# Four short loads of 1, 2, 4 and 8 rows on GpSimd's queue, between the loads of W1 and W2

## The chip, the cores and the metric

One core of a Trainium2 chip. The metric is device time in microseconds (us) of one execution; lower is better. The profile's span is about 1.8 us shorter than that time. Where two kernels are compared, their runs were made on one chip. A run's mean granted TensorE clock is given where it is not 1.00.

## The reference

Linear attention over 8 batches of 8 heads (576 tokens of width 64), then a two-layer feed-forward with ELU:

```python
q_s = softmax(q, axis=-1)            # per token
k_s = softmax(k, axis=2)             # over the sequence
kv  = einsum('bhsd,bhse->bhde', k_s, v)
x   = einsum('bhsd,bhde->bhse', q_s, kv)     # -> 4608 tokens x 512
h   = x @ w_in                               # 512 -> 2048
g   = where(h > 0, h, exp(min(h, 0)) - 1)
out = g @ w_out                              # 2048 -> 512
```

## The kernel before

Tokens go through the feed-forward in nine blocks of 512. W1 and W2 are `w_in` and `w_out`; a unit of q, k or v is four of the eight heads of a batch. In each block, eight "hidden groups" of 256 hidden units are computed on TensorE into four pairs of PSUM banks; ScalarE takes the exp, an engine takes min(exp, 1), VectorE combines both into G and so frees the PSUM pair; then come the output matmuls. A small list scheduler in the program orders each engine's queue by estimated times.

```python
def hg(self, j, g, ps, key, how, kcs=(0, 1, 2, 3)):      # hidden group g of block j
    self.hg_mm(j, g, ps, kcs, key)                       # TensorE into PSUM pair ps
    # ... ScalarE: esb = exp(P) ...
    elif how == "gp":
        S.add("gp", 1120, lambda e: e.tensor_scalar(     # GpSimd: the minimum
            esb[:, :], esb[:, :], 1.0, 0.0, ALU.min, ALU.max), ...)
        S.add("dve", t_dve(1024), lambda e: e.scalar_tensor_tensor(   # VectorE: G, frees P
            gt, esb[:, :], -1.0, P[:, :], ALU.add, ALU.max), ...)
    else:                                                # VectorE: minimum, then G
        S.add("dve", t_dve(1024, 2), lambda e: e.tensor_scalar(...), ...)
        S.add("dve", t_dve(1024), lambda e: e.tensor_tensor(...), ...)

# in program(): GpSimd issues q, k, v of the first units, then W1 (16 pieces), then
for what in (0, "2q", "3q", 1, 2, "2k", "2v", "3k", 3, "3v", 4, 5):
    if isinstance(what, int):
        gp = self.load_w2(what, -50, follow=gp)          # W2 in 6 pieces
    # ... else q, k, v of units 2 and 3 ...

order = [A, Bs, C, Dd]                                   # the four PSUM pairs
for g in range(8):
    self.hg(j, g, order[g % 4], key, "gp" if j or g > 2 else "act" if g == 1 else "dve", ...)
# then the output matmuls; in block 0, W2 piece by piece; the key-value product of
# units 2 and 3 stands in the TensorE queue after the fourth W2 piece
```

In block 0 the minimum of group 3 is the first computing instruction on GpSimd after its loads, and group 7 reuses group 3's PSUM pair. (The four letters A to Dd are PSUM pairs; TensorE's queue is in program order.)

The softmax here doesn't subtract the row's maximum and nothing guards it: scores larger than these inputs give would overflow.

Of the kernel before, what the change touches and what calls it, by code (L numbers as in the profile page):

```python
# [6 lines left out]
F32 = mybir.dt.float32  # L7
# [4 lines left out]
B, H, S, D = 8, 8, 576, 64  # L12
# [245 lines left out]
class Gen:  # L258
# [13 lines left out]
    def alloc(self):  # L272
        nc = self.nc
        a = nc.alloc_sbuf_tensor
        self.ID = a("ID", [128, 128], F16)
        self.IDLE = a("IDLE", [128, 512], F32)
        self.W1 = a("W1", [128, 4, DFF], F32R)
        self.W2 = a("W2", [128, 16, 512], F32R)
        self.GT = a("GT", [128, 16, BLK], F32R)
        self.XT = a("XT", [128, 4, RING], F32R)  # L280
        self.ESB = [a(f"ESB{i}", [128, 1024], F32) for i in range(4)]
        self.OSB = [a(f"OSB{i}", [128, 512], F32) for i in range(4)]
        self.RAW = [{t: a(f"{t.upper()}R{i}", [128, 2, CH, D], F32) for t in "kv"}
                    for i in range(2)]
        self.RQ = [a(f"QR{i}", [128, 2, CH, D], F32) for i in range(4)]
        self.VB = [a(f"VB{i}", [128, 2, CH, D + 1], BF16) for i in range(2)]
        self.QS = [a(f"QS{i}", [128, CH, 128], F16) for i in range(2)]
        self.qsT = [a(f"qsT{i}", [128, CH, 128], F32R) for i in range(2)]
        self.MB = a("MBLK", [128, 2, 2, 128], F32R)
        self.MBLK = [self.MB[:, i, :, :] for i in range(2)]  # L290
        self.ZQ = [a(f"ZQ{i}", [128, 2, CH], F32) for i in range(2)]
        self.RZQ = [a(f"RZQ{i}", [128, 2, CH], F32) for i in range(2)]
        self.RZ = a("RZK", [128, 2, 2], F32)
        self.RZK = [self.RZ[:, i, :] for i in range(2)]
        self.SEEN = a("SEEN", [16, 4, 16], F32)
        self.PS = [nc.alloc_psum_tensor(f"PS{i}", [128, 1024], F32) for i in range(4)]

    def bank(self, i):
# [442 lines left out]
    def program(self):  # L741
        S = self.S
# [5 lines left out]
        for n, h in ((0, 0), (0, 1), (1, 0), (1, 1)):  # L748
# [6 lines left out]
                       follow=gp if eng == "gp" else sp, tag=f"ld q{n}")  # L755
            op.late = 1300 if n == 0 else 2000
            if eng == "gp":
                gp = op
# [4 lines left out]
        for n, t in ((0, "k"), (0, "v"), (1, "k"), (1, "v")):  # L763
            gp = self.load(n, t, "gp", -80, follow=gp)
            gp.late = 2350 if n == 0 else 2200 if t == "k" else 1850
        for s in range(4):
            gp = self.load_w1(s, -60, follow=gp)
# [24 lines left out]
        self.hg_mm(0, 1, 2, (1,))  # L792
        self.ao_rest(0, 1, -60)
        for what in (0, "2q", "3q", 1, 2, "2k", "2v", "3k", 3, "3v", 4, 5):
            if isinstance(what, int):
                gp = self.load_w2(what, -50, follow=gp)
            elif what == "3v":
                for h in range(2):
                    gp = self.load_half(3, "v", h, -50, gp)
            else:  # L800
                gp = self.load(int(what[0]), what[1], "gp", -50, follow=gp)
# [135 lines left out]
```

## Time and profile before

| | before |
|---|---|
| time, median of 2 runs | 298.34 us (298.19 to 298.48) |
| TensorE busy, of a span of 296.5 us | 98% |
| GpSimd: handling of the last load done / first minimum done | 24.84 / 25.93 us |
| TensorE: group 7 / outputs of block 0 / key-value product begin | 27.61 (the prediction worked out 27.53) / 29.43 / 43.07 us |

TensorE sets the end, so only what delays TensorE counts. For a load, the trace of GpSimd gives a start (the issue) and a duration up to the end of its handling on GpSimd. Those ends follow each other one at a time; their distances (0.53 to 0.99 us per load in the kernel before) are the queue's real pace. The prediction shows the lines.

One more line of the waits of the kernel before (who waited for whom: total us, times, longest us) is needed later. The prediction had not used it:

```profile
PEld PS L700 <- DMA W<-in_moe_w_out_dram: 0.4, 1, 0.4
```

It is a weight load of the output matmuls that waited 0.4 us for a piece of W2.

### The profile page before, as it was taken

What the parts mean: (1) busy time and instruction counts of PE and PEld (TensorE: products, weight loads), DVE (VectorE), ACT (ScalarE), POOL (GpSimd) and SP (SyncE); (2) the same over time, 40 slices, a digit from 0 to 9 for tenths busy, and PEclk for the clock granted to TensorE, in tenths of its full rate; (3) what the DMA queues carried; (4) which work ended last, traced back from release to release, by engine and by line L of the source; (5) the groups of instructions that cost most, each with busy time, mean ns of one, the idle gap of its engine ahead of it and who ended that gap; (6) DMA issues with size and microseconds to landing.
All of it is one profiled execution on the core that took longest, in us unless ns stands there. A gap on an engine that the chain in (4) does not pass through costs nothing.

```text
span 296.5 us, 4336 instructions
## 1 busy us (share of the span) xinstructions
PE 290.1 (98%) x1824; PEld 234.9 (79%) x1824; DVE 149.9 (51%) x167; ACT 151.9 (51%) x176; POOL 122.9 (41%) x133
## 2 busy tenths in 40 slices
PE   7999999999999999999999999999999999999995
PEld 2578778887888788878888888888888888888883
DVE  6757942988347903792268416760661056106600
ACT  5666367953676275536554555536531454135411
POOL 8998101662187035713472337314740055005500
PEclk9999999999999999999999999999999999999999
DMA  7999988928991597039902990099003110230022
GB/s 243 320 393 390 389 281 308 389 83 133 337 248 66 200 354 147 0 96 362 238 7 56 359 270 17 4 346 194 0 0 71 45 30 0 56 76 13 0 71 71
DMA packets 36515, 49.37 MB, mean 167 GB/s; under 512 B 16656, under 2 KB 17168, under 8 KB 36496
## 3 DMA queue, kind: packets, MB, share of 16 engines
q1 hardware_dynamic: 29792, 34.29, 40.7%
q0 software_dynamic: 6320, 14.29, 15.8%
q10 hardware_dynamic: 384, 0.53, 0.5%
q8 instruction: 14, 0.23, 0.3%
q14 instruction: 5, 0.04, 0.0%
HBM read 36.70 MB, written 9.44 MB: 156 GB/s over the span
## 4 chain that ended last, share of the span: by engine, by line
PE 84%; DMA 7%; POOL 7%; issue 0%; ACT 0%; DVE 0%; POOLq 0%
PE PS L700 41%; PE PS L654 39%; DMA VR<-in_v_dram 7%; POOL W L347 3%; PE PS L491 2%; PE PS L584 2%; PE PS L618 1%; POOL W L358 1%; POOL KR L315 1%; POOL VR L315 1%; POOL QR L315 0%; POOL QR L753 0%; ACT OSB L714 0%; DVE VB L442 0%; POOL ID L729 0%
## 5 line engine op out<-in xcount | busy, mean ns | idle before, releaser
L683 DVE SCALAR_TENSOR_TENSOR GT<-ESB,PS 128x1024 fp32r<-128x1024 f32 x69 | 84.1, 1221 | 115.7 <-POOL ESB L680 115.5
L700 PE MATMUL PS<-W,GT 128*128 128x512 f32 x576 | 136.5, 392 | 0.0
L654 PE MATMUL PS<-XT,W 128*128 128x512 f32 x576 | 132.9, 390 | 0.0
L654 PEld LDWEIGHTS PS<-XT,W 128*128 128x128 f32 x576 | 107.9, 188 | 22.7 <-DVE GT L676 0.4
L700 PEld LDWEIGHTS PS<-W,GT 128*128 128x128 f32 x576 | 107.0, 188 | 22.4 <-DMA W<-in_moe_w_out_dram 0.4
L680 POOL TENSOR_SCALAR ESB<-ESB 128x1024 f32<-128x1024 f32 x69 | 73.6, 1076 | 101.0 <-ACT ESB L668 101.0
L668 ACT ACTIVATE ESB<-PS 128x1024 f32<-128x1024 f32 x72 | 73.8, 1028 | 51.3 <-PE PS L654 51.3
L714 ACT ACTIVATE OSB<-PS 128x512 f32<-128x512 f32 x36 | 21.4, 600 | 61.3 <-PE PS L700 60.9
L438 POOL CAST VB<-VR 128x1152 bf16<-128x1152 f32 x12 | 14.5, 1210 | 45.4 <-DMA VR<-in_v_dram 45.4
L398 DVE TENSOR_REDUCE ZQ<-QR 128x18 f32<-128x1152 f32 (+1 forms) x18 | 21.8, 1214 | 2.5 <-ACT QR L392 2.5
L412 DVE TENSOR_TENSOR QS<-QR,RZQ 128x1152 f16<-128x1152 f32 x16 | 21.6, 1362 | 0.4
L392 ACT ACTIVATE QR<-QR 128x1152 f32<-128x1152 f32 (+1 forms) x18 | 18.5, 1053 | 2.1 <-DMA QR<-in_q_dram 2.0
L432 ACT ACTIVATE KR<-KR 128x1152 bf16<-128x1152 f32 x14 | 15.9, 1169 | 6.0 <-DMA KR<-in_k_dram 6.0
L425 POOL CAST qsT<-QR 128x1152 fp32r<-128x1152 f16 x12 | 13.8, 1147 | 10.1 <-DMA QR<-QS 10.1
L604 ACT ACTIVATE XT<-PS 128x640 fp32r<-128x640 f32 (+1 forms) x12 | 8.2, 738 | 15.4 <-PE PS L584 15.4
L358 POOL DMA_DIRECT2D W<-in_moe_w_out_dram x6 | 10.2, 2389 | 0.0
L347 POOL DMA_DIRECT2D W<-in_moe_w_in_dram x16 | 10.0, 1361 | 0.0
L640 PE MATMUL PS<-IDLE 128*128 128x512 f32 (+1 forms) x14 | 8.1, 702 | 1.5 <-DVE IDLE L732 1.5
L628 ACT ACTIVATE XT<-PS 128x1024 fp32r<-128x1024 f32 (+3 forms) x8 | 6.8, 846 | 1.1 <-PE PS L618 1.1
L584 PE MATMUL PS<-qsT,MBLK 128*128 128x320 f32 (+3 forms) x32 | 7.1, 338 | 0.0
L640 PEld LDWEIGHTS PS<-IDLE 128*128 128x128 f32 (+1 forms) x14 | 2.6, 211 | 5.5 <-issue 2.3
L491 PEld LDWEIGHTS PS<-VB,KR 64*64 64x64 bf16 x504 | 4.7, 107 | 2.8 <-DVE GT L683 1.8
(45 smaller groups left out, 82.2 us busy)
## 6 DMA issues: line engine op xcount, KB each, us to landing
out_dram<-OSB SPq DMA_DIRECT2D x68, 128.0 KB, 3.6
QR<-in_q_dram SPq DMA_DIRECT2D x12, 576.0 KB, 7.9
KR<-in_k_dram SPq DMA_DIRECT2D x12, 576.0 KB, 5.6
VR<-in_v_dram SPq DMA_DIRECT2D x12, 576.0 KB, 6.6
W<-in_moe_w_in_dram POOLq DMA_DIRECT2D x16, 256.0 KB, 9.5
W<-in_moe_w_out_dram POOLq DMA_DIRECT2D x3, 1024.0 KB, 16.9
KR<-in_k_dram POOLq DMA_DIRECT2D x4, 576.0 KB, 13.6
VR<-in_v_dram POOLq DMA_DIRECT2D x4, 288.0 KB, 14.6
```

Source lines behind the costliest of these rows:

```text
L347: "gp", 530, lambda e, kc=kc: e.dma_start(self.W1[:, kc, sl], w[kc, :, :, sl]), key,
L392: lambda e, part=part: e.activation(part, part, AF.Exp), key,
L398: S.add("dve", 1350 if n > 1 else 750, lambda e, z=z, src=src: e.tensor_reduce(z, src, AX.X, ALU.add), key, R=self.q_res(n) if n > 1 else ...
L412: S.add("dve", 1400, lambda e: e.tensor_tensor(qso, raw[:, :, :, :], rz, ALU.mult), key, R=qR + [f"RZQ{i}"], W=[f"QS{al}"], low=True, tag= ...
L432: S.add("act", t_act(1152, False), lambda e: e.activation(ek[:, :, :, :], flat.rearrange("p (h c d) -> p h c d", h=2, c=CH), AF.Exp), key, ...
L438: self.cv[n] = S.add("gp", 1250, lambda e: e.tensor_copy(VB[:, :, :, 0:D], raw[:, :, :, :]), key, R=rv, W=[f"VB{i}0", f"VB{i}1"], low=True ...
L654: last = e.matmul(P[:, t * 512:(t + 1) * 512], self.W1[:, kc, tt * 128:(tt + 1) * 128], self.XT[:, kc, rc:rc + BLK], start=(kc == 0), stop ...
L668: S.add("act", t_act(1024, True), lambda e: e.activation(esb[:, :], P[:, :], AF.Exp), key, W=[f"E{i}"], X=self.banks(ps), tag=f"exp{j}.{g}")
L680: S.add("gp", 1120, lambda e: e.tensor_scalar(esb[:, :], esb[:, :], 1.0, 0.0, ALU.min, ALU.max), key, X=[f"E{i}"], tag=f"min{j}.{g}", port ...
L683: S.add("dve", t_dve(1024), lambda e: e.scalar_tensor_tensor(gt, esb[:, :], -1.0, P[:, :], ALU.add, ALU.max), key, R=[f"E{i}"], W=gw, X=se ...
L700: last = e.matmul(dst, GT[:, jj, ts * 128:(ts + 1) * 128], self.W2[:, jj, :], start=(jj == 0), stop=(jj == 15))
L714: S.add("act", t_act(512, True), lambda e: e.activation(osb[:, :], src, AF.Copy), key, W=[f"O{i}0", f"O{i}1"], X=[f"b{bk}"], tag=f"evo{jb} ...
```

## The change

The edit adds four small transfers of different shapes on GpSimd's queue, before the first piece of W2. Nobody reads what they bring. It is a probe: what do four loads of next to no bytes do to a kernel whose first 45 us are full of loads?

```diff
@@ alloc
         self.SEEN = a("SEEN", [16, 4, 16], F32)
+        self.ROW = a("ROW", [8, 1152], F32)
@@ program
         for what in (0, "2q", "3q", 1, 2, "2k", "2v", "3k", 3, "3v", 4, 5):
+            if what == 0:
+                for i, (rows, n, at) in enumerate(((1, 384, 0), (2, 320, 384), (4, 256, 704), (8, 192, 960))):
+                    gp = S.add("gp", 600, lambda e, at=at, rows=rows, n=n: e.dma_start(
+                        self.ROW[0:rows, at:at + n], self.w_out[0:rows, 0:n]), -50, W=[f"ROW{i}"],
+                        dma=f"row{i}", nbytes=rows * n * 4, follow=gp, tag=f"row{i}")
             if isinstance(what, int):
                 gp = self.load_w2(what, -50, follow=gp)
```

## The prediction

> **What bounds the kernel now.** I read the page first: engine shares, then the slices, then the chain of work that ended last.
>
> ```profile
> PE 290.1 (98%) x1824; PEld 234.9 (79%) x1824; DVE 149.9 (51%) x167; ACT 151.9 (51%) x176; POOL 122.9 (41%) x133
> GB/s 243 320 393 390 389 281 308 389 83 133 337 248 66 200 354 147 0 96 362 238 7 56 359 270 17 4 346 194 0 0 71 45 30 0 56 76 13 0 71 71
> PE 84%; DMA 7%; POOL 7%; issue 0%; ACT 0%; DVE 0%; POOLq 0%
> ```
>
> TensorE carries the span, with the granted clock full in every slice. After some 45 us nothing holds it: the waits of the window from 45 us to the end give TensorE no wait of its own, and its weight loads sum to 2.2 us over six waits. So time lost before 45 us is not won back, and time lost elsewhere costs nothing. The change sits in the first 45 us, where the loads run at 389 to 393 GB/s in slices 3 to 5 (7.4 us each) and GpSimd issues all of them but two. The timeline of GpSimd, in small windows, shows the issuing. Columns: start, duration, engine, line, what.
>
> ```profile
> 5.69 0.65 POOL L347 DMA_DIRECT2D W<-in_moe_w_in_dram  x1
> ...
> 13.54 2.11 POOL L347 DMA_DIRECT2D W<-in_moe_w_in_dram  x1
> 14.06 2.35 POOL L358 DMA_DIRECT2D W<-in_moe_w_out_dram  x1
> 14.80 2.32 POOL L315 DMA_DIRECT2D QR<-in_q_dram  x1
> ...
> 22.35 2.49 POOL L358 DMA_DIRECT2D W<-in_moe_w_out_dram  x1
> 23.26 2.67 POOL L680 TENSOR_SCALAR ESB<-ESB 128x1024 f32<-128x1024 f32 x1
> ```
>
> Starts and ends differ: the sixteen W1 loads start 0.52 us apart but end 0.62 us apart ((13.54 + 2.11) - (5.69 + 0.65) = 9.31 us over 15). By the last, issue runs 2.11 us ahead of completion. The completions are thus the queue that limits GpSimd, and it never empties until W2's last piece at 22.35 + 2.49 = 24.84 us. The first minimum (of hidden group 3) starts at 23.26 us but takes 2.67 us where its sisters take 1.04: 24.84 + 1.04 = 25.88, near its end at 25.93. It waited for the load queue. This is the place that the change pushes.
>
> Who waits for that minimum? The timelines of VectorE and TensorE, and two of the waits:
>
> ```profile
> 25.97 3.48 DVE L683 SCALAR_TENSOR_TENSOR GT<-ESB,PS 128x1024 fp32r<-128x1024 f32 x3 [1.74 <-POOL ESB L680]
> ```
> ```profile
> 22.06 7.10 PEld L654 LDWEIGHTS PS<-XT,W 128*128 128x128 f32 x32 [0.40 <-DVE GT L676]
> ```
> ```profile
> 29.43 6.78 PE L700 MATMUL PS<-W,GT 128*128 128x512 f32 x28
> 36.04 0.68 PE L464 MATMUL PS<-ID,QS 128*128 128x128 f16 x9
> 36.53 2.98 PE L700 MATMUL PS<-W,GT 128*128 128x512 f32 x12
> 39.35 0.68 PE L464 MATMUL PS<-ID,QS 128*128 128x128 f16 x9
> 39.83 2.98 PE L700 MATMUL PS<-W,GT 128*128 128x512 f32 x12
> 43.07 0.78 PE L491 MATMUL PS<-VB,KR 64*64 64x65 bf16 x72 [0.26 <-DVE VB L442]
> ```
>
> VectorE had idled 1.74 us for GpSimd, then finished group 3 at 25.97 + 1.22 = 27.19 us. By the code, group 7's matmuls take the PSUM pair that this frees. The 32 matmuls of groups 4 to 7 begin at about 22.09 us at 0.227 us each, so group 7 begins at 22.09 + 24 x 0.227 = 27.53 us. The pair was free only 0.34 us earlier; a handover takes 0.05 us (a cast ended at 43.02, its reader began at 43.07), leaving **0.3 us of slack**. TensorE then runs without gaps until 43.07, where it waits 0.26 us for the last half of V of unit 3.
>
> [...] Differences between successive ends give 0.53 to 0.62 us for most loads of 128 pieces (W1, quarter-MB W2, half of V), 0.71 to 0.73 for 256 pieces (q, k, v), 0.76 to 0.99 for 512 (1 MB of W2). It is flat, but half a microsecond per load is not small here.
>
> [...]
>
> **The change part by part.** Nothing is removed. Added are four issues between the last W1 load and the first W2 load, a destination tile of 1152 floats that no one reads, and four semaphores that no one waits for.
>
> 1. Bytes: (384 + 640 + 1024 + 1536) x 4 = 14.3 KB, or 0.04 us at 390 GB/s. [...]
>
> 2. Generation time: from 128 to 256 pieces costs 0.15 us, so about 0.42 us remain for a load of almost no pieces; if the cost is flat below 128 it is 0.55. Four: 1.7 to 2.2 us. I take **1.9 us**. The issue starts shift by about the same.
>
> 3. Transfers: W2's first piece is issued 1.9 us later. It needed 13.4 us from issue to landing at 14.06 us, waiting behind W1:
>
> ```profile
> W<-in_moe_w_out_dram POOLq DMA_DIRECT2D x1, 1024.0 KB, 13.4
> W<-in_moe_w_in_dram POOLq DMA_DIRECT2D x3, 256.0 KB, 11.0
> ```
>
> A 1 MB load is 2.7 us of transfer at 390 GB/s, so most of those 13.4 us are backlog. The queue does not run dry when issue slips 1.9 us. The landings of W2, q, k, v of units 2 and 3 stay put to 0.1 us, including V at 42.5 us.
>
> 4. GpSimd's first minimum ends 1.9 us later, at 27.8. VectorE's group 3 ends at 29.1. Group 7 begins at 29.15 instead of 27.53: TensorE loses 1.9 - 0.3 = 1.6 us. It ends at about 31.0. Group 4's evacuation is done at about 30.3 and group 5's near 31.5, ahead of the output tiles that need those banks (31.0 and 32.8), so no second loss follows.
>
> 5. TensorE reaches the key-value product 1.6 us late, where it waited 0.26 us for V, which lands when it did: about 0.3 us come back. Net **1.3 us**, kept to the end: 298.34 + 1.3 = 299.64, rounded to 299.7 for small matters of item 1.
>
> 6. VectorE from 30.0 to 38.1 us is nearly full, with groups 6 and 7 and the softmax of q for units 2 and 3. It starts 1.9 us late and regains some of it in its former waits; the transposes at 36.04 and 39.35 us also move 1.6 us later, with 0.8 and 1.2 us spare before (the products end at 35.2 and 38.1). I expect no new wait.
>
> **The rivals.**
>
> A. Hidden. The shift is absorbed, as GpSimd is busy only 41% overall and no one reads the new tile: 298.3. For it: deep backlog of transfers. Against: the 1.74 us wait of VectorE for GpSimd right behind the loads, and only 0.3 us of slack.
>
> B. Small loads are dear to generate[...]. For: nothing measured; against: the flatness of the other loads.
>
> C. [...] If the 17 us from 27.5 to 44.5 grew by 5%, V and W2's tail would land 0.85 us later; with TensorE already 1.3 us late this is still hidden. Only over 8% would add to the sum, and 15% would make 301.0.
>
> D. Another order. The program sorts each engine's queue by estimated times, and the four loads enter it at 0.6 us each. A low-priority exp or reduction on ScalarE or VectorE may go ahead of an urgent one; one displaced softmax step is 1.2 to 1.4 us on those engines. It might cost up to that on TensorE, or save a part of the loss: 299 to 301.
>
> **Range and chances.** Generation between 0.3 and 0.55 us gives a loss of 0.6 to 1.6 us; rivals B and D stretch it upward. So 298.6 to 301.5 holds it 8 times in 10, around 299.7. Two per cent is 6 us: slower by that needs 1.7 us per small load or a lost overlap, 3%. Faster by 2% would need TensorE work to vanish, 1%. Within 2%: 96%.
>
> **What would show it.** Between the last W1 and the first W2 completion on GpSimd stand four issues of 0.4 to 0.55 us each; the first minimum ends near 27.8 us; VectorE's wait before its group 3 grows from 1.74 to about 3.6 us; the weight loads or matmuls before group 7 show a wait of about 1.6 us for VectorE; the output matmuls begin near 31.0 us; the 0.26 us wait at the key-value product is gone; V still lands near 42.5 us; the rest is the same, later. It is wrong if the first minimum moves by under 1 or over 3 us, if the loads land later by over 1 us, or if TensorE shows new waits after 45 us.

1.9 us on GpSimd, less 0.3 of slack, less 0.3 given back at V, is 1.3 us, so 298.34 + 1.3 = 299.64, put at 299.7. Gone are an allowance in item 1 that only the rounding up could draw on, the size of rival B (an assumption, measured nowhere, from which the range took a part of its upper end) and the cause that rival C gave for slower transfers; the shares by which C lets them slow are assumed. "Generation", here and in the expectations, is the time between the ends of two loads that follow each other on GpSimd; what GpSimd does in that time was not shown.

## The result and the profile after

299.24 us (299.19 to 299.28, 2 runs) against 298.34: a ratio of 1.0033, 95% interval 1.0009 to 1.0057, about +1.0 us. Ratios here are the mean time of one kernel's fast runs over that of the other's of the same rounds, so they differ a little from the ratio of the medians. By the 2% rule this is "the same"; the interval says that it is a small loss. It lies within the predicted range of 298.6 to 301.5, 0.5 us under the predicted 299.7.

GpSimd's timeline after (lines moved down by one in the file, from the new tile on):

```profile
13.57 2.13 POOL L348 DMA_DIRECT2D W<-in_moe_w_in_dram  x1
14.09 2.12 POOL L798 DMA_DIRECT2D ROW<-in_moe_w_out_dram  x1
...
15.61 2.10 POOL L798 DMA_DIRECT2D ROW<-in_moe_w_out_dram  x1
16.10 2.40 POOL L359 DMA_DIRECT2D W<-in_moe_w_out_dram  x1
...
24.52 2.07 POOL L359 DMA_DIRECT2D W<-in_moe_w_out_dram  x1
25.26 2.42 POOL L681 TENSOR_SCALAR ESB<-ESB 128x1024 f32<-128x1024 f32 x1
```

The last W1 load ends at 15.70, the last short load at 17.71: 2.01 us for four, **0.50 us each**. The queue ends at 26.59 (24.84 before), the first minimum at 27.68 (25.93). VectorE and TensorE, after:

```profile
27.71 4.61 DVE L684 SCALAR_TENSOR_TENSOR GT<-ESB,PS 128x1024 fp32r<-128x1024 f32 x4 [3.66 <-POOL ESB L681]
```
```profile
28.99 2.11 PE L655 MATMUL PS<-XT,W 128*128 128x512 f32 x8 [1.44 <-DVE GT L684]
30.94 6.51 PE L701 MATMUL PS<-W,GT 128*128 128x512 f32 x28
37.29 0.68 PE L465 MATMUL PS<-ID,QS 128*128 128x128 f16 x9
...
43.99 0.78 PE L492 MATMUL PS<-VB,KR 64*64 64x65 bf16 x72
```

The bracket on TensorE is new: group 7 waits 1.44 us for VectorE, which waited 3.66 us (1.74 before) for GpSimd. Now take the lag of each row against the kernel before: group 7 +1.38 us (28.99 against 27.61), outputs +1.51 (after the pause the eight matmuls took 1.95 us to the first output, before 1.82), first transpose +1.25 (37.29 against 36.04), key-value product +0.92 (43.99 against 43.07). The loss shrinks in two places. The first 28 output matmuls took 6.51 us instead of 6.78: that is the wait for W2 shown above, gone. And the wait of 0.26 us before the key-value product is gone. From there on the lag stays (the spans differ by 297.4 - 296.5 = 0.9 us). The chain that ended last names the same links (start, us, what):

```profile
15.69 2.01 POOL ROW L798 x4
...
25.33 1.26 POOL W L359 x2
26.59 1.10 POOL ESB L681
...
27.71 1.23 DVE GT L684
...
28.99 2.11 PE PS L655 x8
```

### The profile page after: what moved, and what is told of

It reads as the page before. It is cut to its first block, busy times and chain, and to the rows that moved or that the text cites. A ratio compares the mean times of both kernels' runs of the same rounds, so it can differ in the third digit from the quotient of the medians.

```text
span 297.4 us, 4340 instructions
## 1 busy us (share of the span) xinstructions
PE 289.4 (97%) x1824; PEld 234.7 (79%) x1824; DVE 149.6 (50%) x167; ACT 152.1 (51%) x176; POOL 124.7 (42%) x137
## 4 chain that ended last, share of the span: by engine, by line
PE 89%; POOL 9%; DVE 0%; issue 0%; ACT 0%; POOLq 0%
PE PS L701 45%; PE PS L655 40%; POOL W L348 3%; PE PS L492 2%; PE PS L585 2%; POOL W L359 1%; PE PS L619 1%; POOL KR L316 1%; POOL ROW L798 1%; POOL VR L316 1%; POOL QR L316 1%; POOL QR L754 0%; DVE GT L684 0%; POOL ESB L681 0%; POOL VR L337 0%
## 5 line engine op out<-in xcount | busy, mean ns | idle before, releaser
L641 PE MATMUL PS<-IDLE 128*128 128x512 f32 (+1 forms) x14 | 7.4, 632 | 1.9 <-DVE IDLE L733 1.5
```

## The experiments

Theory: each short load costs GpSimd half a microsecond of handling whatever its rows; this delays the first minimum, the freeing of a PSUM pair and group 7; waits for transfers later give about 0.6 us back. Rivals: the bytes or the odd row counts cost; a later arrival of W2 and V costs; the program's own scheduler reordered something. All twelve runs gave correct results; "GpSimd" below is the end of the first minimum, "group 7" the start of its matmuls, both from the profiled run.

| kernel | median, us | before, us | ratio (95%) | GpSimd | group 7 |
|---|---|---|---|---|---|
| the change (first result) | 299.24 | 298.34 | 1.0033 (1.0009-1.0057) | 27.68 | 28.99 |
| two loads | 298.35 | 298.04 | 1.0006 (0.9994-1.0017) | 26.86 | 28.17 |
| eight loads | 303.05 | 298.04 | 1.0160 (1.0144-1.0176) | 29.50 | 30.82 |
| rows on SyncE | 298.00 | 298.04 | 0.9998 (0.9985-1.0012) | 25.71 | no wait |
| rows behind W2 | 299.43 | 298.04 | 1.0045 (1.0031-1.0060) | 27.91 | 29.22 |
| order of before | 298.88 | 297.86 | 1.0034 (1.0021-1.0046) | 27.57 | 28.88 |
| 16 rows each | 298.86 | 297.86 | 1.0031 (1.0017-1.0045) | 27.51 | 28.82 |
| group 3 on VectorE, change | 298.01 | 297.86 | 1.0001 (0.9989-1.0014) | | no wait |
| group 3 on VectorE, before | 297.73 | 297.86 | 0.9993 (0.9981-1.0006) | | no wait |

### How many loads: two and eight

```diff
-  enumerate(((1, 384, 0), (2, 320, 384), (4, 256, 704), (8, 192, 960)))
+  enumerate(((4, 256, 704), (8, 192, 960)))                  # two
+  enumerate(((1, 384, 0), ..., (8, 192, 960)) * 2)           # eight; the second four into rows 8 to 15 of a taller tile
```

> Only the loads of 4 and 8 rows, on GpSimd's queue. Theory (generation time of about 0.5 us per load on GpSimd, TensorE held at group 7): the first minimum ends near 26.7 us, about 1 us earlier than with four; TensorE loses about 0.4 us before group 7, and the two waits for transfers that the kernel before had (0.6 us) swallow it: 298.3 to 298.5, no change from before. Rival (cost in proportion to the number of loads): half of +0.9, so 298.8. Rival (the load of one row alone is what costs): 298.3 too, but with the first minimum where it was before.

> The four loads twice over, eight in all. Theory: the queue of GpSimd ends 4 us later than before, the first minimum near 29.7 us, group 7 at about 31.0 us where it began at 27.5; 3.5 us lost, 0.6 given back: +2.9 us, about 301.2. Rival (in proportion): +1.8, about 300.1. Rival (a one-off[...]): +0.9, 299.2.

Two loads cost 0.0006 x 298 = 0.2 us, an interval that includes none. The minimum moved by 0.93 us and group 7 waited:

```profile
28.17 2.11 PE L655 MATMUL PS<-XT,W 128*128 128x512 f32 x8 [0.84 <-DVE GT L684]
...
43.17 0.78 PE L492 MATMUL PS<-VB,KR 64*64 64x65 bf16 x72
```

Yet the key-value product begins at 43.17 (43.07 before). Half the loads don't cost half the loss: the waits for transfers swallow the first 0.6 us.

Eight loads were my clearest miss: +4.8 us, not +2.9. GpSimd did as expected (29.50 for "near 29.7"; eight loads in 3.94 us, 0.49 each), and group 7 too (30.82 for "about 31.0"). But then:

```profile
30.82 3.58 PE L655 MATMUL PS<-XT,W 128*128 128x512 f32 x8 [2.50 <-DVE GT L684]
34.24 6.55 PE L701 MATMUL PS<-W,GT 128*128 128x512 f32 x28
```

Eight matmuls took 3.58 us instead of 2.11. Stretches of the same profile (busy times of the engines, then the granted TensorE clock, the third number from the end):

```profile
29.00:30.00 1.00, 0.00 (x0) 0.00 (x0) 0.46 (x1) 0.97 (x2) 1.00 (x4) 1.00 1.33 389
...
31.00:32.00 1.00, 1.00 (x3) 0.81 (x4) 1.00 (x2) 1.00 (x1) 1.00 (x2) 0.50 1.38 387
...
33.00:34.00 1.00, 1.00 (x4) 0.71 (x4) 1.00 (x2) 0.00 (x0) 0.00 (x0) 0.50 1.46 398
34.00:35.00 1.00, 1.00 (x6) 0.82 (x5) 1.00 (x2) 0.56 (x1) 0.00 (x0) 0.98 1.18 392
```

After a pause of 2.5 us TensorE was granted half its clock until 34.03 us. That is 1.5 us more. For the profiled run the sum then closes: 3.2 at group 7, plus 1.5, less 0.6, is 4.1 us, and it took 302.29 - 298.04 = 4.25 us more. The other three runs took 0.7 to 1.1 us longer still; no profile shows where. The section "More pauses" below looks at when the clock changes. All four runs of this kernel have a mean clock of 0.994. The changed kernel's pause of 1.44 us left the clock full.

### The bytes or the engine that issues them: rows on SyncE

```diff
-  gp = S.add("gp", 600, lambda e, ...: e.dma_start(...), ..., dma=f"row{i}", follow=gp, ...)
+  sp = S.add("sp", 600, lambda e, ...: e.dma_start(...), ..., dma=f"orow{i}", follow=sp, ...)
```

(The name with an o makes the program wait for them at its end.)

> The same four loads issued by SyncE, GpSimd's queue as before. Theory: the cost is GpSimd's time, not the bytes or the reads: 298.3, GpSimd's first minimum at 25.9 us. Rival (the transfers themselves disturb the DMA engines): +0.5 or more. The rows travel early here, before the W2 loads, so this does not exclude a disturbance that only loads from GpSimd make.

298.00 against 298.04: no cost; the first minimum ends at 25.71 and V is waited for again (0.22 us). The bytes are not it.

### Where the queue is delayed: rows behind W2

```diff
         for what in (0, "2q", ...):
-            if what == 0: ... the four loads ...
         self.ldq, self.w2 = None, [gp]
+        ... the four loads, after the last piece of W2 ...
```

> The four loads behind the last W2 load instead of ahead of the first. Theory: the first minimum waits for the same number of generations: the same as the changed kernel, +0.9, 299.2, and W2 lands as before or earlier. Rival (the delay of W2's and V's loads is what costs): 298.3.

+1.3 us, as high as the change or higher (the intervals overlap). W2's issues are not delayed at all here, so a late arrival of W2 or V can't be the cause. Here the minimum moved by the full 1.98 us, against 1.75 with the loads in front. The 0.23 us between is taken up below.

### The order of the queues, and the shape of the loads

Set beside the kernel before, the change also moved one reduction on VectorE and one cast on GpSimd by two places near 55 us. To take that away, the loads are counted at 1 ns in the scheduler's estimate; the queues then have the order of before:

```diff
-                    gp = S.add("gp", 600, lambda ...
+                    gp = S.add("gp", 1, lambda ...
```

> The four loads as in the change, but counted at 1 ns each in the program's own ordering of its queues, so that every engine's queue is in the order of the kernel before, save for the four loads. Theory: +0.9, 299.2. Rival (the displaced reduction on VectorE and cast on GpSimd near 55 us matter): nearer to 298.3.

The ratio is 1.0034, that of the change. The order is not it. And with 16 rows per load and the same bytes:

```diff
-  ((1, 384, 0), (2, 320, 384), (4, 256, 704), (8, 192, 960))
+  ((16, 24, 0), (16, 40, 24), (16, 64, 64), (16, 96, 128))
```

> Four loads of 16 rows each with the same bytes as the short ones[...]. Theory (fixed generation time, whatever the rows): +0.9, 299.2, 0.5 us per load in GpSimd's queue. [...]

(A rival: if the odd row counts cost, the time would be near 298.3.)

The ratio is 1.0031, 1.96 us for the four (0.49 each). The odd row counts are not it: one row or sixteen, a load takes GpSimd half a microsecond.

### Taking the link out: group 3's minimum on VectorE

```diff
-  self.hg(j, g, ..., "gp" if j or g > 2 else "act" if g == 1 else "dve", ...
+  self.hg(j, g, ..., "gp" if j or g > 3 else "act" if g == 1 else "dve", ...
```

> The changed kernel with the minimum of hidden group 3 moved from GpSimd to VectorE, which had been idle there for 3.7 us. Theory: group 7 no longer waits; the whole 0.9 us goes: 298.3, with the waits for W2 and V back. Rival (something else in the load queue costs): stays near 299.2.

> The kernel before with the same move. Theory: nothing to gain, as TensorE had 0.3 us of slack there and then waits for W2 and V anyway: 298.3, within 0.2 us. If the group 3 hand-over had a hidden cost before, this is faster by up to 0.5 us.

With the four loads and this edit, 298.01 against 297.86, ratio 1.0001: the whole loss is gone, though the loads are still issued. TensorE has no pause before group 7, and the two waits are back:

```profile
29.20 6.70 PE L701 MATMUL PS<-W,GT 128*128 128x512 f32 x28
...
42.74 0.78 PE L492 MATMUL PS<-VB,KR 64*64 64x65 bf16 x72 [0.22 <-DVE VB L443]
```

The same edit on the kernel before gives 0.9993, with 1 inside the interval: no gain shown, so no version that beats both. In the kernel before, the transfers hold TensorE next: 0.27 us for W2 in the first outputs and 0.26 us for V.

### More pauses: six loads, and eight with group 3 on VectorE

```diff
+  enumerate((..., (8, 192, 960), (1, 384, 0), (2, 320, 384)))   # six
   # and: the eight loads with the edit of the last section
```

> Six short loads (the four, then those of one and two rows again). With eight, TensorE's clock fell to half after a pause of 2.5 us, which no theory had counted. Theory with the clock holding: GpSimd's first minimum ends near 28.8 us, group 7 begins near 30.2 instead of 27.5, 2.6 us lost, 0.6 given back, +2.0 us (300.1), pause of about 2 us. If a pause of 2 us is enough to halve the clock: 1.5 us more, +3.5 (301.6).

> The kernel of six short loads once more, for a profile: of its six runs, five took 301.7 to 302.3 us, while the profiled one took 300.5 and had its slow clock at the start instead. Theory: in a profile of the usual kind TensorE pauses about 2 us before group 7 and then runs group 7 and the first outputs at half clock for some 3 us, and the time is about 301.8. Rival: the usual runs lose those 1.5 us elsewhere, and the clock after the pause is full.

> Eight short loads with the minimum of group 3 on VectorE. Theory: GpSimd's first minimum is now that of group 4, ends near 29.5 us as with eight loads, and its evacuation at about 30.8 releases the first output bank; group 7 is not held, the outputs begin near 30.9 instead of 29.4: 1.5 us lost, 0.6 given back, +0.9 (298.9), the pause 1.4 us and the clock full. If the halved clock came from the loads and not from the pause, the clock falls here too and the time is above 300.

Six loads, eight runs. One run with a full clock took 299.98, against 297.94 for the kernel before: +2.0, the theory's sum. Five took 301.7 to 302.3 at a mean clock of 0.994. Two took 300.5 (clock 0.992 and 0.994), and as luck had it, both of them were the profiled ones. These show neither reading of mine. In both, as the stretch of the second one's profile below has it with a clock of 0.66, TensorE had its slow clock between 10 and 15 us, long before group 7, and began the main part of block 0 at 19.3 us instead of 16.4, so that group 7 did not wait at all.

```profile
10.00:15.00 5.00, 5.00 (x35) 2.43 (x35) 3.25 (x7) 2.83 (x4) 5.00 (x12) 0.66 1.20 342
```

The two traces show how that came about. SyncE's second load of q, issued at 1.21 us as in every kernel, landed at 6.14 us; in the other profiles it landed at 4.3 to 4.6 us, and with eight loads at 5.43. TensorE therefore waited for VectorE's softmax twice, 1.05 and 1.00 us, before 9.38 us, and then ran at half clock (10.37 to 13.78 us in the first of the two). No short load is issued before 14.0 us, so none had a part in this. Why the load of q landed late stays open.

Where the five slower runs lost some 1.7 us more (their 302.0 - 298.3 against that 2.0) is therefore not shown; their mean clock is that of the eight-load runs, which is an argument and no more. The kernel before has a run of 301.62 us at a clock of 0.987 too; it has no profile, so whether it started late in the same way is not shown.

Eight loads with group 3 on VectorE: I expected 298.9 and a pause of 1.4 us. Measured: 300.18 and 300.19 in two runs with a clock of 0.998 or more, and 301.7 to 302.0 in four at 0.992 to 0.994. The profile is of the slower kind. Its pause is longer than I thought, and comes at the first output:

```profile
31.77 8.25 PE L701 MATMUL PS<-W,GT 128*128 128x512 f32 x28 [2.19 <-DVE GT L684]
```

28 matmuls took 8.25 us instead of 6.51, at a clock of 0.50 between 32 and 35 us. Group 7 was not held, as expected; the halved clock follows the pause and not group 7. My question was whether pause or loads halve the clock. This profile had both, but two runs of the same kernel kept a clock of 0.998 or more with all eight loads, and the six-load profiles had the half clock before any short load. So the loads as such are not it.

The moments at which the granted clock changes, found with ever narrower windows, say more. In the four profiles with a half clock they lie whole multiples of 3.41 us apart (with eight loads: up at 6.73, down at 30.62, up at 34.03), and each half lasts 3.41 us. In the traces of the kernel before and of the change, the clock table has it full from 6.33 to 296.47 us and from 4.53 to 298.07, 85 and 86 times 3.413 us. In the 3.41 us that ended with the fall to half clock, TensorE had been idle for 2.30 us (eight loads: its pause began at 28.32), 2.19 (this kernel) and 2.04 and 2.06 us (six loads, the two waits together). Cut into the same windows from the first rise of the clock on, the ten other profiles have at most 1.59 us of idle time in one (rows at the head). So here 2.04 us of idle time in one window was followed by half the clock and 1.59 was not; between these nothing was measured. That a pause of 2.2 us across the border of two windows is split, and leaves the clock full, would fit the two kinds of run of this kernel, 1.5 us apart. It is the author's reading and was not shown: a second profile of this kernel was not taken.

Why was the pause 0.8 us longer than expected (2.19 us, not 1.4)? GpSimd's queue ended at 29.37 instead of 28.42 with the same loads. Ends of three loads in this kernel, then VectorE's minimum operations:

```profile
20.36 2.93 POOL L359 DMA_DIRECT2D W<-in_moe_w_out_dram  x1
21.10 2.95 POOL L359 DMA_DIRECT2D W<-in_moe_w_out_dram  x1
21.84 3.17 POOL L316 DMA_DIRECT2D KR<-in_k_dram  x1
```
```profile
22.32 0.72 DVE L688 TENSOR_SCALAR ESB<-ESB 128x1024 f32<-128x1024 f32 x1 [0.41 <-ACT ESB L669]
...
24.21 0.69 DVE L688 TENSOR_SCALAR ESB<-ESB 128x1024 f32<-128x1024 f32 x1
```

The loads end at 23.29, 24.05 and 25.01. The first (the load ahead of it ended at 22.20) took 1.09 us, the second 0.76, the third 0.96; with eight loads alone they took 0.77, 0.75 and 0.71. The two long ones are those beside which VectorE ran its minimum from and to SBUF. So was a short load beside VectorE's minimum at 18.67 us, with 0.79 us instead of 0.48; the three together are 0.9 us. In some runs the load lengthens (0.2 to 0.3 us), in others VectorE's operation does (1.15 and 1.01 us instead of 0.69 with the rows behind W2, where beside the second a load took 0.84 instead of 0.53 as well). What ties the two together was not shown. In the kernel before, two loads were long in this way (0.98 and 0.72 us, where 0.75 and 0.54 are usual) beside VectorE's operations at 18.65 and 22.28 us. In the changed kernel, none was. That fits the 0.26 us by which the changed kernel's queue caught up (2.01 us of short loads, but an end only 1.75 us later). No run tested this alone, so this is argued from these durations.

### No backlog to hide behind: rows at the head of the queue

```diff
+        ... the four loads, ahead of the first q load on GpSimd ...
         for n, h in ((0, 0), (0, 1), (1, 0), (1, 1)):
```

> The four short loads ahead of everything that GpSimd issues, where no backlog of transfers hides them. Theory: every landing of its queue moves by up to 2 us, the first minimum by 2 us: TensorE starts its real work later and the kernel loses 1 to 2 us, 299.3 to 300.3, with V of unit 3 landing 1 to 2 us later than 42.5. Rival (issue time is hidden wherever it stands): +0.9 as in the change and V on time.

301.04 us (300.31 to 301.60, 4 runs) against 298.34: ratio 1.0086 (1.0037 to 1.0134), more than expected. TensorE has no pause before group 7, but it starts late, and V is late as well:

```profile
18.96 12.95 PE L655 MATMUL PS<-XT,W 128*128 128x512 f32 x56
...
44.83 0.78 PE L492 MATMUL PS<-VB,KR 64*64 64x65 bf16 x72
```

VectorE began to convert V's last half at 44.31 us, 1.76 later than the 42.55 of before. At the head hardly anything is waiting for the DMA engines yet (the short loads landed 2.5 to 3.4 us after their issue; behind W1 it was 9.6 to 10.6), so the 2 us of issue become 1.8 us of arrival; behind W1, the same 2 us moved V's conversion from 42.55 to 42.35, that is, not at all. This kernel also changed ScalarE's order in the first microseconds, so the size of its loss is not the issue's alone. The profile is of the fastest of its four runs (300.31).

## Why the prediction was right, and where it was off

- **Steps 1 and 3, bytes and transfers**: right. V's arrival did not move by more than 0.2 us, and that earlier; SyncE's rows cost nothing (298.00 against 298.04).
- **Step 2, generation**: right. 0.50 us per load, inside 0.42 to 0.55; four took 2.01 us for the 1.9 taken.
- **Step 4, the chain over group 3 to group 7**: right in every link. First minimum 27.68 for 27.8, group 3 done at 28.93 for 29.1, group 7 at 28.99 for 29.15, outputs at 30.94 for 31.0. TensorE lost 1.38 us at group 7 and 1.51 by the outputs, where I had 1.6; moving the one minimum removed it all. Two things here were not known beforehand. In the kernel before, group 7 began at 27.61 and not at 27.53, as the first matmul of group 4 took 0.31 us, so the slack was 0.37 us and not 0.3. And 27.8 came so near in part by luck: the loads took 0.1 us more than I had, and 0.26 us was caught up behind them.
- **Step 5, what comes back**: the term that was mis-sized. I gave 0.3 us, the wait for V alone, and wrote that TensorE "runs without gaps until 43.07". It did not: the first 28 output matmuls held 0.27 us of waiting for W2's second piece. The waits had the line. The profile of before had said the same in another way: that piece, the middle one of three at 16.9 us from issue to landing, issued at 16.22, landed at 33.1 us, and the seventeenth output matmul was due at 29.43 + 16 x 0.227 = 33.06. The measured return was 1.51 - 0.92 = 0.6 us. With 1.5 - 0.6 the sum is 0.9 instead of 1.3, which is nearly the whole difference.
- **Step 6 and rival D**: no new wait on VectorE or ScalarE held TensorE, and the two displaced instructions cost nothing. Rival A (hidden) is right for two loads and wrong for four. Rival B (dear small loads) fell (0.50 us each), and rival C (slower transfers afterwards) found no support: V's last half was converted from 42.35 us on, before from 42.55. Nor did the odd row counts: four loads of sixteen rows cost the same (1.0031 against 1.0033).
- **Slower than 2%**: I wrote that it needs 1.7 us per short load or a lost overlap. A load took 0.5 us. The runs with other numbers of loads show besides that the loss isn't in proportion to their handling: 0.2, 1.0 and 4.8 us for two, four and eight. It has a threshold at the low end (the waits of 0.6 us) and the halved clock at the high end.

## What to carry to other kernels

Here a load cost GpSimd half a microsecond (0.49 to 0.50 us) even if it carried almost nothing, and GpSimd's next computing instruction waited for all loads queued before it (its end moved from 25.93 to 27.68 us with four). Before calling a load hidden, ask who computes next on that engine, and how soon someone needs the buffer that this frees; then subtract every wait further on, including those inside a merged row of matmuls, since a delay that ends in an existing wait is partly free (here 0.6 us). Keep TensorE's pauses short: in these runs 1.44 us cost 1.5, while 2.5 cost 4, the halved clock included.
